# Seven half-size products in place of eight for the gate and value matmuls of an attention + two-MLP kernel

## The chip, the cores and the metric

One core of a Trainium2 chip runs the whole program. The metric is the device time of one execution in microseconds (us); a kernel's time is the median of several executions. TensorE (PE in the profile) does the matmuls, VectorE (DVE) and ScalarE (ACT) the elementwise work, and SyncE (SP) issues every DMA on one queue, in order.

## The reference

```python
# attention: x (4, 8, 512, 64), state (4, 8, 32, 64), scale 1/8
a = softmax(scale * x @ state.T);   xread = a @ state
a2 = softmax(scale * state @ x.T);  sread = a2 @ x
y = concatenate([xread, sread]) -> 2176 rows of 512

# first MLP, d_ff 2048
h = y @ w_in;  y = (h * tanh(softplus(h))) @ w_out

# second MLP, d_ff 1536
xn = y / sqrt(mean(y * y) + 1e-6) * rms_g
g, v = xn @ w_gate, xn @ w_val
out = (silu(g) * v) @ w_out2
```

The weights lie in DRAM as 64-bit floats.

## The kernel before

Rows are worked on in chunks: chunks 0 to 3 are the 512 read rows of one batch each, and chunk 4 holds the 128 state rows. Activations lie transposed in SBUF (features on partitions, rows along the free dimension), four tiles of 128 features to a chunk.

Every matmul operand is an fp16 pair, a high half and a low half, and a product of two such operands is three fp16 matmuls (high by high, high by low, low by high). One output tile of 128 features by 512 rows over 512 input features is therefore 12 matmuls of 128x512. The code calls 512 columns of the hidden dimension a unit `u` (four for the first MLP, three for the second), and 128 of them an `f`.

- **Weights.** `fetch` (L514 to L550) loads half a unit of raw 64-bit words into a staging tile (1 MB to a DMA) and turns them into fp32 with a scaled copy (L449 or L453), a sign (L534), low bits (L539 or L541) and a join (L550). `norms` (L563) sums squares on ACT, `pow2` sends the sum through a one-column matmul with `ones` (L462) and computes a power-of-two scale in six small DVE steps (L468 to L473), and `split` writes the high half (L449 or L453) and the low half (L579). The value and gate weights (`whole`) are scaled by `rms_g` and prepared while the first MLP runs; they then stay in SBUF.
- **First MLP.** `group` gives, for each `f`, 12 matmuls (L869), the activation on ACT (L880), and the split of its result (high half L449 or L453, low half on DVE L884). `l2` follows one pair of `f` later: four pieces of 6 matmuls (L902) accumulate into four PSUM banks.
- **Second MLP.** `rms` normalizes a chunk. `gated` gives for each `f` 12 gate and 12 value matmuls (L991) into two PSUM banks, SiLU on ACT (L1000), the product with the value on DVE (L1002), and the split (L451 or L449, then L1006). `l3` (L1020) multiplies the result with `w_out2`.
- **PSUM.** Four banks `p` rotate for everything that is computed, four banks `a` hold the accumulations of `l2` and `l3`.

The order of the work is not the order of the code. Each step is an `op` with its engines, its estimated cost, what it reads and writes, and for matmuls a time `at` by which it is due; `Plan.order` simulates the engines and buffers forward and backward a few times and keeps the best order. What comes out is one fixed instruction stream for each engine, and each engine works through its stream strictly in order.

Of the kernel before, what the change touches and what calls it, by code (L numbers as in the profile page):

```python
# [21 lines left out]
XEXP = 15  # L22
TABLES = {
# [7 lines left out]
class Op:  # L31
    __slots__ = (
        "engs", "fn", "deps", "succ", "bufs", "tab", "at", "due", "reserve", "lat", "name")


class Plan:
# [15 lines left out]
    def __init__(self, nc):  # L52
        self.nc = nc
# [14 lines left out]
    def op(self, engs, fn, r=(), w=(), tab=None, at=None, reserve=0, lat=0.0, after=(), due=None, name=""):  # L68
        o = Op()
        o.engs, o.fn, o.tab, o.at, o.due, o.reserve, o.lat, o.name = engs, fn, tab, at, due, reserve, lat, name  # L70
        o.succ, o.bufs = [], []
# [68 lines left out]
    def chains(self):  # L140
# [7 lines left out]
        for o in reversed(self.ops):  # L148
            cost = min(o.engs.values())
            cost = cost + o.lat if "T" in o.engs else (1.0 if "D" in o.engs else self.SPARE) * cost + o.lat  # L150
            t = min(x for x in (o.at, o.due, 1e9) if x is not None)
            t = min([t, *(late[after[b]] - cost for b in o.bufs if b in after)])
            late[o] = min([t, *(late[s] - cost - 0.14 for s in o.succ)])
# [161 lines left out]
def attn_moe_moe_kernel(  # L315
# [27 lines left out]
    wts = ctx.enter_context(tc.tile_pool(name="wts", bufs=1))  # L343
    slots = ctx.enter_context(tc.tile_pool(name="slots", bufs=1))
    wk = ctx.enter_context(tc.tile_pool(name="wk", bufs=1))
    psum = ctx.enter_context(tc.tile_pool(name="psum", bufs=1, space=PSUM))
    att = ExitStack()
    att_p = att.enter_context(tc.tile_pool(name="att", bufs=1, side="right"))
# [21 lines left out]
    tiles = {}  # L370
    for u in range(U1):
        tiles["wi", u] = wts.tile([128, 4, 512], F32, name=f"win{u}")
        tiles["wo", u] = wts.tile([128, 4, 512], F32, name=f"wout{u}")
    for u in range(U2):
        tiles["wg", u] = wts.tile([128, 4, 512], F32, name=f"gate{u}")
        tiles["w2", u] = tiles["wi", u]
    spare = {w: wts.tile([128, 2, 512], F16, name=f"spare_{w}") for w in ("wi", "wo")}
    stage0 = wts.tile([128, 4, 512], F32, name="stage0")
    slot = [slots.tile([128, KD, 512], F32, name=f"slot{c}") for c in range(B)]
    slot.append(slots.tile([128, KD, B * NS], F32, name="slot4"))  # L380
    slot += [tiles["wg", 1], tiles["wg", 2]]
    width = [S] * B + [B * NS]
# [6 lines left out]
    P.fifo.update(("s", "g", "xb", "xt", "t2", "t3", "sbt"))  # L389
    P.pool("s", [wk.tile([128, 2, 512], F32, name=f"s{k}") for k in range(3)])  # L390
    P.pool("g", [wk.tile([128, 2, 2, 512], F16, name=f"g{k}") for k in range(3)])
    P.pool("sx", [wk.tile([128, 512], F32, name=f"sx{k}") for k in range(2)])
    P.pool("junk", [wk.tile([128, 2, 512], U8, name="junk")])
    P.pool("raw", [stage0, tiles["wg", 0]])
    P.pool("xb", [att_p.tile([128, 4, DM], F32, name="xb")])
    P.pool("xt", [att_p.tile([128, 2, 512], F32, name=f"xt{k}") for k in range(2)])
    P.pool("t2", [att_p.tile([128, 512], F32, name=f"t2{k}") for k in range(4)])
    P.pool("t3", [att_p.tile([128, 512], F32, name=f"t3{k}") for k in range(2)])
    P.pool("sbt", [att_p.tile([128, 2, 2, 128], F32, name="sbt")])
    sb = att_p.tile([128, B, 2, 4, D], F32, name="sb")  # L400
    srt = slot[B]
    P.pool("raw2", [])
    att_tiles = [0]
# [13 lines left out]
    def place(c, d):  # L417

        return reg("wg", c - B, d) if c > B else [("slot", c, d)]

    def reg(w, u, k):

        w = "wi" if w == "w2" else w
        return [(w, u, 2 * k), (w, u, 2 * k + 1)]

    def where(w, u, k, a):

        if a:  # L430
            return w, u, k, 0
        if k > 1:
            return w, u, k - 2, 1
        return ("wv", U2 - 1, k + 2, 1) if (w, u) == ("wg", 0) else (w, u - 1, k + 2, 1)

    def part(w, u, k, a):
        w, u, k, h = where(w, u, k, a)
        return half(tiles[w, u])[:, k, h, :] if u >= 0 else spare["wi" if w == "w2" else w][:, k - 2, :]

    def part_name(w, u, k, a):  # L440
        w, u, k, h = where(w, u, k, a)
        return reg(w, u, k)[h]

    def parts(w, u, ks):
        return [part_name(w, u, k, a) for k in ks for a in range(2)]
# [12 lines left out]
    def pow2(part, pname, k, floor, nm):  # L458
# [8 lines left out]
        def fn(e):  # L467
            nc.vector.tensor_scalar(t, P[b][:, :k], floor, 2.0, ALU.max, ALU.mult)  # L468
            nc.vector.tensor_scalar(q, t.bitcast(I32), 24, None, ALU.logical_shift_right)
            nc.vector.tensor_scalar(z, q, -1, 190 + XEXP, ALU.mult, ALU.add)  # L470
            nc.vector.tensor_scalar(s.bitcast(I32), z, 23, None, ALU.logical_shift_left)
            nc.vector.tensor_scalar(q, q, 64 - XEXP, None, ALU.add)
# [29 lines left out]
    def fetch(w, u, pool="raw", after=()):  # L502

        if not wide:
            op({"D": 2.95}, lambda e: nc.sync.dma_start(out=tiles[w, u], in_=source(w, u)),
               w=[n for k in range(4) for n in reg(w, u, k)], lat=1.9, after=after, name=f"load {w}{u}")
            return
        for v in range(2):
            r = buf(fresh("raw"), pool)

            def raw(r=r):
# [4 lines left out]
                w=[r, *reg(w, u, 2 * v), *reg(w, u, 2 * v + 1)], lat=1.9, after=after, name=f"load {w}{u}{v}")  # L516
            for j in range(2):
                k = 2 * v + j
                g = reg(w, u, k)

                def hi(e, raw=raw, j=j, k=k):
                    a = raw()[:, j, :].bitcast(F32).rearrange("p (f w) -> p f w", w=2)[:, :, 1]
                    copy_to(e, tiles[w, u][:, k, :], a, 2.0 ** -112)

                last = op({"A": a_sb(512), "V": v2(512)}, hi, r=[r], w=g, after=after, name=f"hi {w}{u}{k}")
# [22 lines left out]
                def join(e, k=k, q=q):  # L548
                    ti = tiles[w, u][:, k, :].bitcast(I32)
                    nc.vector.scalar_tensor_tensor(  # L550
                        ti, ti, 3, P[q].bitcast(I32), ALU.logical_shift_left, ALU.bitwise_or)

                op({"V": v1(512)}, join, r=[q, (q, "s"), (q, "l"), *g], w=g, name=f"join {w}{u}{k}")

    def norms(w, u, part, pname, gain=None):

        step = 1 if gain is not None else 2
        for k in range(0, 4, step):
            q = buf(fresh("junk"), "junk")

            def fn(e, k=k, q=q):
                jk = P[q][:, :step, :]
                nc.scalar.activation(  # L563
                    jk, tiles[w, u][:, k:k + step, :], ACTF.Square,
                    scale=1.0 if gain is None else gain[:, k:k + 1],
                    accum_out=part[:, k // step:k // step + 1])

            op({"A": a_sb(512 * step) + 0.17}, fn,
               r=["rg", *(n for j in range(step) for n in reg(w, u, k + j))], w=[q, (pname, k)], name=f"sq {w}{u}{k}")

    def split(w, u, scale, sname):

        for k in range(4):
            g = reg(w, u, k)
            hn, ln = part_name(w, u, k, 0), part_name(w, u, k, 1)
            op({"A": a_sb(512) + 0.09, "V": v2(512) + 0.06}, lambda e, k=k: copy_to(
                e, part(w, u, k, 0), tiles[w, u][:, k, :], scale(k)),
# [575 lines left out]
```

## Time and profile before

| | |
|---|---|
| median of 3 runs | 832.39 us (832.09 to 832.92) |
| profiled execution, its own time | 832.4 us |
| its span, first to last instruction | 830.6 us |
| TensorE busy | 805.8 us, 97% of the span |
| VectorE busy | 452.4 us, 54% |
| ScalarE busy | 344.2 us, 41% |
| mean granted TensorE clock | 0.989 of full speed |
| DMA | 45.26 MB, 54 GB/s over the span |

The span and the time differ by 1.8 us, which lies around the instructions. A busy time is the union of the instructions' durations on one engine. Matmuls overlap in the records, so a matmul's pace is the time of a long run of them divided by their number, not the duration of one.

### The profile page before, as it was taken

The numbers are of one execution on the slowest core, as the hardware profiler recorded it, in microseconds if no ns is written. First come the engines' busy times: TensorE is split into PE (matmuls) and PEld (weight loads), VectorE is DVE, ScalarE is ACT, GpSimd is POOL, SyncE is SP. The second block draws the span as 40 slices with busy tenths as digits, with TensorE's granted clock in tenths as the row PEclk, the third lists the DMA queues.
The fourth block names the chain that finished last, engine by engine and source line by source line (L and its number), as shares of the span: only waits on it lengthen the run. The fifth ranks groups of instructions, "written<-read, shape, count | busy, mean of one in ns | idle before, by whom it ended". The sixth has DMA issues, their size and how long they took to land.

```text
span 830.6 us, 10926 instructions
## 1 busy us (share of the span) xinstructions
PE 805.8 (97%) x4486; PEld 393.7 (47%) x4486; DVE 452.4 (54%) x962; ACT 344.2 (41%) x582; POOL 1.6 (0%) x7
## 2 busy tenths in 40 slices
PE   7689999999999999999999999999999999999996
PEld 4334444444445448644444444444444444444474
DVE  5899987459275688558884271324333352312231
ACT  5999995135152499448752140103113130100010
POOL 0000000000000000000000000000000000000000
PEclk9799999999999999999999999999999999999999
DMA  8711861000000177213100000100010000100001
GB/s 215 204 52 54 284 221 52 1 1 0 1 1 1 51 253 254 102 51 102 51 0 1 1 1 0 52 1 1 0 45 7 1 0 1 51 1 0 1 2 64
DMA packets 28517, 45.26 MB, mean 54 GB/s; under 512 B 19124, under 2 KB 19124, under 8 KB 27956
## 3 DMA queue, kind: packets, MB, share of 16 engines
q1 hardware_dynamic: 28468, 44.57, 16.4%
q8 instruction: 35, 0.57, 0.3%
q14 instruction: 14, 0.11, 0.0%
HBM read 40.11 MB, written 4.46 MB: 54 GB/s over the span
## 4 chain that ended last, share of the span: by engine, by line
PE 90%; ACT 5%; DVE 3%; SPq 1%; issue 1%; DMA 0%; ACTq 0%
PE p L991 32%; PE a L902 20%; PE p L869 19%; PE a L1020 16%; PE p L698 1%; ACT t L449 1%; ACT L282 1%; ACT slot L449 1%; ACT sx L539 1%; PE p L685 0%; SPq L653 0%; PE p L945 0%; ACT junk L563 0%; DMA xb<-in_x_dram 0%; ACT win L449 0%
## 5 line engine op out<-in xcount | busy, mean ns | idle before, releaser
L902 PE MATMUL a<-g,wout 128*128 128x512 f16 (+1 forms) x880 | 174.3, 347 | 0.0
L869 PE MATMUL p<-slot,win 128*128 128x512 f16 (+1 forms) x880 | 173.0, 347 | 0.0
L1002 DVE SCALAR_TENSOR_TENSOR s<-s,page,p 128x512 f32<-128x512 f32 x51 | 38.1, 747 | 217.2 <-PE p L991 217.2
L991 PE MATMUL p<-slot,val 128*128 128x512 f16 (+1 forms) x720 | 150.0, 347 | 0.0
L1000 ACT ACTIVATE s<-p,page 128x512 f32<-128x512 f32 x51 | 35.0, 686 | 263.3 <-PE p L991 263.2
L1020 PE MATMUL a<-win,g 128*128 128x512 f16 x544 | 136.5, 379 | 0.0
L991 PE MATMUL p<-slot,gate 128*128 128x512 f16 (+1 forms) x640 | 129.4, 347 | 0.0
L869 PEld LDWEIGHTS <-win 128*128 128x128 f16 x880 | 79.0, 98 | 83.3 <-issue 0.8
L902 PEld LDWEIGHTS <-wout 128*128 128x128 f16 x880 | 79.0, 98 | 81.9 <-issue 1.3
L991 PEld LDWEIGHTS <-val 128*128 128x128 f16 x720 | 65.2, 98 | 68.2
L1020 PEld LDWEIGHTS <-g 128*128 128x128 f16 x612 | 59.7, 98 | 72.3 <-issue 1.7
L880 ACT ACTIVATE s<-p,page 128x512 f32<-128x512 f32 x68 | 46.1, 680 | 99.5 <-PE p L869 99.5
L991 PEld LDWEIGHTS <-gate 128*128 128x128 f16 x640 | 57.7, 98 | 60.6
L453 DVE TENSOR_SCALAR g<-s,page 128x512 f16<-128x512 f32 x52 | 25.1, 483 | 60.9 <-ACT s L880 60.6
L884 DVE SCALAR_TENSOR_TENSOR g<-s,page,g 128x512 f16<-128x512 f32 x68 | 50.9, 748 | 4.4 <-ACT g L449 2.6
L1006 DVE TENSOR_TENSOR g<-s,g 128x512 f16<-128x512 f32 x51 | 35.3, 692 | 1.8 <-ACT g L449 0.2
L539 ACT ACTIVATE sx<-stage 128x512 uint16<-128x512 uint16 x41 | 31.1, 775 | 0.1
L282 ACT ACT_TABLE_LOAD x21 | 26.9, 1283 | 0.4
L449 ACT ACTIVATE slot<-a,page 128x512 f32<-128x512 f32 (+2 forms) x21 | 13.9, 676 | 24.5 <-PE a L1020 18.6
L534 DVE TENSOR_SCALAR sx<-stage 128x512 uint16<-128x512 uint16 x52 | 21.4, 455 | 4.0 <-DMA stage<-in_moe_w_val_dram 1.8
L1020 PE MATMUL a<-spare_wi,g 128*128 128x512 f16 x68 | 23.0, 379 | 0.0
L902 PE MATMUL a<-g,spare_wo 128*128 128x512 f16 (+1 forms) x80 | 20.8, 347 | 0.0
(176 smaller groups left out, 697.3 us busy)
## 6 DMA issues: line engine op xcount, KB each, us to landing
stage<-in_moe_w_out_dram SPq DMA_DIRECT2D x10, 1024.0 KB, 4.9
stage<-in_moe_w_val_dram SPq DMA_DIRECT2D x6, 1024.0 KB, 5.0
stage<-in_moe_w_gate_dram SPq DMA_DIRECT2D x6, 1024.0 KB, 5.0
stage<-in_moe_w_in_dram SPq DMA_DIRECT2D x4, 1024.0 KB, 5.5
gate<-in_moe_w_in_dram SPq DMA_DIRECT2D x4, 1024.0 KB, 6.3
gate<-in_moe_w_out_dram SPq DMA_DIRECT2D x4, 1024.0 KB, 5.1
out_dram<-slot SPq DMA_DIRECT2D x4, 1024.0 KB, 4.0
xb<-in_x_dram SPq DMA_DIRECT2D x24, 128.0 KB, 3.7
```

The source lines that it names most:

```text
L282: self.nc.scalar.preload_act_table_set(TABLES[table])
L449: nc.scalar.activation(o, i, ACTF.Copy, scale=1.0 if scale is None else scale)
L539: nc.scalar.activation(s16[:, :, 0], r16[:, :, 1], ACTF.Copy, scale=2.0 ** -13, bias=2.0 ** -14 - 0.5)
L869: nc.tensor.matmul(P[ph][:, i * n:(i + 1) * n], part("wi", u, k, a)[:, f * 128:(f + 1) * 128], xh[:, k, b, :], start=m == 0, stop=m == 3 * ...
L880: op({"A": a_ps(512) + 0.09}, lambda e, s=s, q=q, ph=ph, ce=ce: nc.scalar.activation(P[s][:, q, :], P[ph], ACTF.Mish, scale=ce), r=[ph, s, ...
L884: op({"V": v1(512) + 0.06}, lambda e, q=q, s=s, g=g, u=u: nc.vector.scalar_tensor_tensor(P[g][:, q, 1, :], P[s][:, q, :], rho[u], P[g][:, ...
L902: nc.tensor.matmul(P[ya[d]][:, :n], part("wo", u, f, a)[:, d * 128:(d + 1) * 128], P[g][:, q, b, i * n:(i + 1) * n], start=first and m == ...
L991: nc.tensor.matmul(P[p][:, i * n:(i + 1) * n], part(w, u, k, a)[:, f * 128:(f + 1) * 128], xh[:, k, b, :], start=m == 0, stop=m == 3 * KD - 1)
L1000: op({"A": a_ps(512) + 0.09}, lambda e, s=s, pg=pg: nc.scalar.activation(P[s][:, 0, :], P[pg], ACTF.Silu, scale=c3), r=[pg, "c3"], w=[s], ...
L1002: op({"V": v1(512) + 0.06}, lambda e, s=s, pv=pv: nc.vector.scalar_tensor_tensor(P[s][:, 0, :], P[s][:, 0, :], kap, P[pv], ALU.mult, ALU.m ...
L1006: op({"V": v1(512)}, lambda e, s=s, g=g: nc.vector.tensor_tensor(P[g][:, 0, 1, :], P[s][:, 0, :], P[g][:, 0, 0, :], ALU.subtract), r=[s], ...
L1020: nc.tensor.matmul(P[oa[t]], P[g][:, 0, a, o:o + 128], part("w2", u, f, b), start=first and m == 0, stop=last and m == mm - 1)
```

## The change

For chunks 0 to 3, `gated` now computes gate and value of a unit as a product of two 2x2 block matrices. The blocks of the activations are 256 features by 256 rows, those of the weights 256 features by 256 hidden columns. The scheme needs seven products where the plain one needs eight, and sums of blocks before and after. The new function `quad` issues it: seven products of 12 matmuls of 128x256 each, collected in three PSUM banks `A`, `B_` and `C`, with one copy out of PSUM and five additions on DVE (L1100) into tiles of pool `t`. A bank takes its next product only when the addition that reads it is done.

```diff
+        product(A, "A11", W11, True)
+        op({"A": a_ps(512) + 0.09, "V": v1(512) + 0.06}, lambda e: copy_to(e, P[a1], P[A]), r=[A], w=[a1], name=f"{w} a1")
+        product(B_, "S2", T2, True)
+        add(u2, B_, a1)
+        product(C, "S1", T1, True)
+        product(A, "A12", W21)
+        product(B_, "S3", T3)
+        add(u3, B_, a1)
+        add(u3, C, u3)
+        product(B_, "A22", T4)
+        add(a1, B_, a1)
+        product(C, "S4", W22)
+        add(u2, C, u2)
+        return A, u2, a1, u3
```

One product:

```diff
+                for f in range(2):
+                    for k in range(2):
+                        for a, b in ((0, 0), (0, 1), (1, 0)):
+                            nc.tensor.matmul(
+                                P[to][:, f * 256:f * 256 + 256],
+                                part(w, u, j, a)[:, k * 256 + f * 128:k * 256 + f * 128 + 128], h[:, k, b, :],
+                                start=begin and (f, k, a, b) == (0, 0, 0, 0),
+                                stop=(f, k, a, b) == (1, 1, 1, 0), skip_group_check=True)
```

The activations' sums are made in `rms`, four subtractions or additions on DVE for each chunk, and seven blocks are split into halves where four tiles were. Chunk 4 is computed plainly as before (`gated_last`, L1166).

The weights' sums are made once. `seven` takes the place of `whole` for gate and value: it applies `rms_g`, makes four sums, and splits eight tiles of a unit where four were split. Each unit has a scale of its own. Since eight tiles of six units don't fit beside the rest, each prepared unit is written to DRAM and read back when the space of the first MLP's weights is free:

```diff
+        for k in range(4):
             op({"A": a_sb(512) + 0.09, "V": v2(512) + 0.06}, lambda e, k=k: copy_to(
+                e, dst(k), dst(k), rg[:, k:k + 1]), r=["rg"], w=dn(k), name=f"gain {w}{u}{k}")
...
+        s = norms([(both(W11, W12), qn(W11, W12)), (both(W21, W22), qn(W21, W22))], (w, u), XW, f"{w}{u}")
+        for t, a, b in ((T1, W12, W11), (T3, W22, W12), (T2, W22, T1), (T4, W21, T2)):
+            op({"V": v1(512)}, lambda e, t=t, a=a, b=b: nc.vector.tensor_tensor(q(t), q(a), q(b), ALU.subtract),
+               r=qn(a, b), w=qn(t), name=f"sum {w}{u}{t}")
+        for j in range(8):
+            split(m, at, j, s, ((w, u), "s"), f"{w}{u}")
...
+    def keep(w, u, after):
+        P.spare = KEEP
+        n = 2048 if w == "w2" else 4096
+        t = dram.tile([128, n], F32, name=f"kept_{w}{u}")
+        kept[w, u] = t
+        if w == "w2":
+            plain(w, u, prep, 0, XEXP, "raw2", after)
+        else:
+            seven(w, u, prep, 0, "raw2", after)
+        op({"D": n / 690}, lambda e: nc.sync.dma_start(out=t[:, :], in_=prep(0, n)),
+           r=prep.names(0, n), w=[("kept", w, u)], lat=1.9, name=f"keep {w}{u}")
...
+        op({"D": n / 690}, lambda e: nc.sync.dma_start(out=m(at, n), in_=kept[w, u][:, :n]),
+           r=[("kept", w, u)], w=m.names(at, n), lat=1.9, after=after, name=f"back {w}{u}")
```

SBUF is laid out anew as a few large regions (`Mem`), with dependencies kept by 1 KB pieces. All nine late units are prepared in one region, `prep`, and through one staging tile (there were two). The first MLP's work is put in another sequence: attention of chunk 2 moves behind most of the work on chunks 0 and 1, and the order of the chunks changes.

```diff
-        attention(2, T0 + DUE2)
...
-        group(0, 0, [0], None, B + 1)
-        group(1, 1, [0], None, B + 2)
-        group(2, 2, [0], None, 3)
...
+        group(0, 0, [0], None, 2)
+        group(1, 1, [0], None, 3)
+        group(2, 0, [1], 2, 2)
+        group(3, 1, [1], 3, 3)
+        group(4, 0, [2, 3], 2, 0)
+        flush()
+        attention(2, clock[0] + DUE2)
+        group(5, 1, [2, 3], 3, 1)
+        flush()
         attention(3, clock[0] + DUE3)
...
+        for u in range(U2):
+            for w in ("wg", "wv"):
+                keep(w, u, [bar])
+        for u in range(U2):
+            keep("w2", u, [bar])
...
+        group(6, 2, every, None, 2)
+        flush()
+        rms(0, slots_xe[0], [conv, done])
+        group(7, B, every, None, B)
+        group(8, 3, every, None, 3)
```

How the streams move is shown at three places. The first is DVE in the middle of the first MLP, where value and gate weights are prepared. `psm` is the region of `prep`, `page` holds scales, `g` and `tt` belong to the first MLP's results. Before, while units of `val` are made:

```order
L550 SCALAR_TENSOR_TENSOR val_2300<-val_2300,sx_109 128x512
L453 TENSOR_SCALAR g_107<-s_104,page_137 128x512
L884 SCALAR_TENSOR_TENSOR g_107<-s_104,page_137,g_107 128x512
L534 TENSOR_SCALAR sx_110<-stage_89 128x512
L534 TENSOR_SCALAR sx_109<-stage_89 128x512
L541 TENSOR_SCALAR sx_110<-stage_89 128x512
L550 SCALAR_TENSOR_TENSOR val_2301<-val_2301,sx_110 128x512
```

With the change, the end of one unit's sums and its scale:

```order
L918 SCALAR_TENSOR_TENSOR g<-tt,page_116,g 128x512
L544 TENSOR_SCALAR sxm<-psm 128x512 x2
L459 TENSOR_SCALAR psm<-psm 128x2x256
L551 TENSOR_SCALAR sxm<-psm 128x512
L560 SCALAR_TENSOR_TENSOR psm<-psm,sxm 128x2x256 x2
L918 SCALAR_TENSOR_TENSOR g<-tt,page_116,g 128x512
L638 TENSOR_TENSOR psm<-psm 128x512 x2
L578 TENSOR_TENSOR page_110<-page_110 128x1
L638 TENSOR_TENSOR psm<-psm 128x512
L474 TENSOR_SCALAR page_110<-p_84 128x1
```

The subtractions L638 are new, and between the sum of squares (L578) and the scale (L474) stands the one-column matmul on PE, at a fixed place of PE's stream.

The second is DVE in the second MLP. Before, one `f` after the other, with a step of `rms` between:

```order
L1002 SCALAR_TENSOR_TENSOR s_105<-s_105,page_138,p_98 128x512
L940 TENSOR_TENSOR rms_2296<-rms_2296,rms_2297 128x512
L1006 TENSOR_TENSOR g_108<-s_105,g_108 128x512
L1002 SCALAR_TENSOR_TENSOR s_103<-s_103,page_138,p_97 128x512
L451 CAST g_106<-s_103 128x512
L1006 TENSOR_TENSOR g_106<-s_103,g_106 128x512
```

With the change (`p_83` to `p_86` are the four banks, `tt` the tiles of pool `t`):

```order
L1138 TENSOR_TENSOR g<-tt,g 128x512 x3
L457 COPY tt<-p_84 128x512
L1100 TENSOR_TENSOR tt<-p_85,tt 128x512 x2
L1100 TENSOR_TENSOR tt<-p_83,tt 128x512
L1100 TENSOR_TENSOR tt<-p_85,tt 128x512
L1100 TENSOR_TENSOR tt<-p_83,tt 128x512
L457 COPY tt<-p_86 128x512
L1100 TENSOR_TENSOR tt<-p_84,tt 128x512
```

The copy and the additions stand between products that reuse the same bank.

The third is SP's queue. Before, raw weights alternate between two staging tiles (`stage_89`, and `gate_84` or later `stage_2303`):

```order
L514 DMA stage_89<-in_moe_w_in_dram 128x2x1024
L514 DMA gate_84<-in_moe_w_in_dram 128x2x1024
L514 DMA stage_89<-in_moe_w_out_dram 128x2x1024
L514 DMA gate_84<-in_moe_w_out_dram 128x2x1024
L514 DMA stage_89<-in_moe_w_val_dram 128x2x1024
L514 DMA stage_2303<-in_moe_w_val_dram 128x2x1024
```

With the change (`kept_` names are in DRAM):

```order
L525 DMA psm<-in_moe_w_gate_dram 128x2x1024 x2
L525 DMA psm<-in_moe_w_val_dram 128x2x1024
L1241 DMA kept_wg_106<-psm 128x4096
L525 DMA psm<-in_moe_w_val_dram 128x2x1024
L525 DMA psm<-in_moe_w_gate_dram 128x2x1024
L1241 DMA kept_wv_107<-psm 128x4096
L525 DMA psm<-in_moe_w_gate_dram 128x2x1024
```

A unit's write to DRAM stands in the same queue between the loads of the next unit's two halves.

## Rows read from the trace of the kernel before

**Rows 1.** The page: span, busy time of each engine, share of the chain by engine.

```profile
span 830.6 us, 10926 instructions
PE 805.8 (97%) x4486; PEld 393.7 (47%) x4486; DVE 452.4 (54%) x962; ACT 344.2 (41%) x582; POOL 1.6 (0%) x7
PE 90%; ACT 5%; DVE 3%; SPq 1%; issue 1%; DMA 0%; ACTq 0%
```

**Rows 2.** Busy time by stretch: stretch and its length, then each engine's busy time.

```profile
core 0: us, PE busy (x) PEld busy (x) DVE busy (x) ACT busy (x) POOL busy (x), PEclk, DMA share, GB/s
0.00:14.00 14.00, 10.96 (x64) 7.54 (x64) 4.15 (x8) 4.79 (x11) 1.59 (x7) 0.88 0.72 187
14.00:122.20 108.20, 94.30 (x608) 45.83 (x609) 99.55 (x241) 101.34 (x185) 0.00 (x0) 0.95 0.55 166
...
420.00:791.00 371.00, 371.00 (x1717) 168.50 (x1716) 136.16 (x232) 75.53 (x112) 0.00 (x0) 1.00 0.02 9
...
799.00:815.00 16.00, 16.00 (x253) 14.47 (x251) 5.17 (x8) 2.75 (x4) 0.00 (x0) 1.00 0.17 68
```

**Rows 3.** The chain that ended last, second MLP: start us, length us, what.

```profile
783.34 2.59 PE p L991 x12
...
809.60 5.36 PE p L991 x96
814.96 7.78 PE a L1020 x36
```

**Rows 4.** Groups by form: busy us, mean ns of one, then idle before.

```profile
L991 PEld LDWEIGHTS <-val 128*128 128x128 f16 x720 | 65.2, 98 | 68.2
...
L1002 DVE SCALAR_TENSOR_TENSOR s<-s,page,p 128x512 f32<-128x512 f32 x51 | 38.1, 747 | 217.2 <-PE p L991 217.2
L1006 DVE TENSOR_TENSOR g<-s,g 128x512 f16<-128x512 f32 x51 | 35.3, 692 | 1.8 <-ACT g L449 0.2
L453 DVE TENSOR_SCALAR g<-s,page 128x512 f16<-128x512 f32 x52 | 25.1, 483 | 60.9 <-ACT s L880 60.6
L550 DVE SCALAR_TENSOR_TENSOR win<-win,sx 128x512 int32<-128x512 int32 x28 | 18.4, 684 | 0.9 <-ACT sx L539 0.3
...
L483 DVE TENSOR_SCALAR page<-page,page 128x1 f32<-128x1 f32 x52 | 8.9, 202 | 0.0
...
L563 ACT ACTIVATE junk<-win 128x1024 uint8<-128x1024 f32 x14 | 14.7, 1052 | 3.5 <-DVE win L550 3.5
L449 ACT ACTIVATE win<-win,page 128x512 f16<-128x512 f32 x18 | 12.6, 719 | 7.6 <-DVE win L579 7.5
L449 ACT ACTIVATE win<-stage 128x512 f32<-128x512 f32 x19 | 12.2, 671 | 0.0
```

**Rows 5.** Timeline of PE, start of the first MLP: start us, length us, instructions.

```profile
42.30 0.66 PE L685 MATMUL p<-ident,xb 128*128 128x128 f32 x4
...
50.78 0.60 PE L869 MATMUL p<-slot,spare_wi 128*128 128x512 f16 x2
```

**Rows 6.** Timeline of DVE, the scale of the third weight unit.

```profile
102.70 0.16 DVE L468 TENSOR_SCALAR page<-p 128x1 f32<-128x1 f32 x1
```

**Rows 7.** DMA issues: KB each, us to landing.

```profile
stage<-in_moe_w_val_dram SPq DMA_DIRECT2D x6, 1024.0 KB, 5.0
...
out_dram<-slot SPq DMA_DIRECT2D x4, 1024.0 KB, 4.0
```

**Rows 8.** Timeline of all engines: a hand-over from PE to DVE.

```profile
658.00 2.75 PE L991 MATMUL p<-slot,val 128*128 128x512 f16 x12
...
660.59 0.81 PE L1020 MATMUL a<-win,g 128*128 128x512 f16 x3
660.86 0.75 DVE L1002 SCALAR_TENSOR_TENSOR s<-s,page,p 128x512 f32<-128x512 f32 x1 [5.82 <-PE p L991]
```

**Rows 9.** Timeline of all engines: a hand-over from DVE to a waiting PE.

```profile
83.88 0.75 DVE L753 SCALAR_TENSOR_TENSOR slot<-p,page,slot 128x512 f16<-128x512 f32 x1
...
84.69 0.65 PE L771 MATMUL p<-xb,t 128*32 128x64 f32 x32 [0.38 <-DVE slot L753]
```

More of the change, by code (lines that the diff above doesn't have):

```diff
@@ L415, in bank, with sl_names, part, part_names @@
         return buf(fresh("bank"), pool)
[L417 to L445, printed above, removed]
+    def sl_names(c, d):
+        return slotm[c].names(d * width[c], width[c])
+    def part(w, u, j, a):
+        m, at = rest[w, u] if j == 7 else (home[w, u][0], home[w, u][1] + 512 * j)
+        return m(at + 256 * a, 256, F16)
+    def part_names(w, u, js):
+        m, at = home[w, u]
+        return [n for j in js for n in (rest[w, u][0].names(rest[w, u][1], 512) if j == 7 else m.names(at + 512 * j, 512))]
     def copy_to(e, o, i, scale=None):
@@ L548, in join @@
                 def join(e, k=k, q=q):
-                    ti = tiles[w, u][:, k, :].bitcast(I32)
+                    ti = dst(k).bitcast(I32)
                     nc.vector.scalar_tensor_tensor(
[L551 to L558, printed above, removed]
+                        ti, ti, 3, two(P[q].bitcast(I32)), ALU.logical_shift_left, ALU.bitwise_or)
@@ L644, in attention @@
         if b == 1:
-            xb, xbl = "x1", [n for k in range(KD) for n in place(3, k)]
+            xb, xbl = "x1", [n for k in range(KD) for n in sl_names(3, k)]
             P.place[xb] = slot[3]
@@ L964, in rms @@
[L964 to L982 removed]
+            to = y[:, d, :] if c < B else t(d % 2)
@@ new lines, in quad, with product, fn, add @@
+    def quad(c, u, w):
+        A, B_, C = bank(), bank(), bank()
+        a1, u2, u3 = (buf(fresh(k), "t") for k in ("a1", "u2", "u3"))
+        blk = xblk[c]
+        def product(to, xn, j, begin=False, end=False):
+            h, hn = blk[xn]
+            def fn(e):
+                for f in range(2):
[6 more added lines that the diff above has]
+                                stop=(f, k, a, b) == (1, 1, 1, 0), skip_group_check=True)
+            cost = pe(256, 12)
+            op({"T": cost}, fn, r=[*hn, *part_names(w, u, [j])], w=[to, *(["l1"] if begin else [])],
+               at=clock[0], name=f"{w} c{c} u{u} {xn}")
+            clock[0] += cost
+        def add(to, bank_, a):
+            op({"V": v1(512) + 0.06}, lambda e: nc.vector.tensor_tensor(P[to], P[bank_], P[a], ALU.add),
+               r=[bank_, a], w=[to], name=f"{w} add")
+        product(A, "A11", W11, True)
[12 more added lines that the diff above has]
+        return A, u2, a1, u3
@@ L1019, in fn @@
                     for a, b in ((0, 0), (0, 1), (1, 0)):
                         nc.tensor.matmul(
-                            P[oa[t]], P[g][:, 0, a, o:o + 128], part("w2", u, f, b),
-                            start=first and m == 0, stop=last and m == mm - 1)
+                            P[oa[t]], P[g][:, a, o:o + 128], part("w2", u, f, b),
+                            start=first and m == 0, stop=last and m == 11)
                         m += 1
-            cost = pe(512, 3 * len(fs))
@@ L1026, in l3 @@
-            op({"T": cost}, fn, r=[g, *parts("w2", u, fs)], w=[oa[t]], at=clock[0], name=f"l3 c{c} u{u}")
+            cost = pe(512, 12)
+            rd = gs[t // 2 * 2:t // 2 * 2 + 2] if c < B else gs
+            op({"T": cost}, fn, r=[*rd, *part_names("w2", u, range(4))], w=[oa[t]], at=clock[0], name=f"l3 c{c} u{u}")
             clock[0] += cost
@@ new lines, in attn_moe_moe_kernel @@
+        load("wg", 0, [done])
+        load("wv", 0, [done])
+        for u in range(U2):
+            load("w2", u, [conv])
+        gated_scales()
+        group(6, 2, every, None, 2)
+        flush()
+        rms(0, slots_xe[0], [conv, done])
+        group(7, B, every, None, B)
+        group(8, 3, every, None, 3)
+        flush()
+        for u in range(1, U2):
+            load("wg", u)
+            load("wv", u)
+        rms(1, slots_xe[1])
+        gated(0)
+        rms(2, slots_xe[0])
```

522 lines of the change are left out of this document (312 added, 210 removed).

## The prediction

> **What bounds the kernel now.** I began with the page. TensorE is busy for 97% of the span, and 90% of the chain that ended last is PE [rows 1]. A busy PE need not be a PE at its peak, so the next view was busy time by stretch [rows 2]: from 420 to 791 us PE is busy in every microsecond at the full granted clock, while DVE is busy for 136 of 371 us and ACT for 76. The second MLP is bound by PE alone. The start is another matter. From 14 to 122 us DVE is busy for 99.6 of 108.2 us (92%) and ACT for 101.3, and PE, at 94.3, has only just enough to do. The reader should keep both stretches in mind: the change takes work from PE in the second and adds work to DVE, part of it in the first. The chain then gives PE's paces [rows 3]: 12 matmuls of 128x512 in 2.59 us, 215.8 ns each, and 96 of 128x128 in 5.36 us, 55.8 ns each. Each of these matmuls loads weights of its own; a load lasts 98 ns [rows 4], longer than the 55.8 ns between two matmuls, so the loads lie beside the matmuls.
>
> The profiled execution took 832.4 us with a span of 830.6, and the median of the runs is 832.39: the sum below starts from 832.4 and needs no correction.
>
> **What PE saves: 28.5 us.** Removed are 4 chunks x 3 units x 2 weights x 4 `f` x 12 = 1152 matmuls of 128x512, 248.6 us at 215.8 ns. Added are 4 x 3 x 2 x 7 products x 12 = 2016 of 128x256. No steady run of that width is in the trace. The two paces of [rows 3] lie on a line of 0.4167 ns a column plus 2.5 ns, which gives 109.2 ns at 256 columns and 220.1 us. As PE was never idle there, all 28.5 us are on the path. Everything else on PE has the same count as before.
>
> The Trainium skill, page "TensorE: Matmul & The Clock Gate", section "Back-to-back issue gap", states about 81 ns for each pair of weight load and matmul at 128 columns, 25 ns above its figure without the load. By an estimate from that page, 25 ns on each of the 2016 narrow matmuls would cost 50 us and turn the gain into a loss of 22. The trace disagrees: 55.8 ns at 128 columns, loads included [rows 3].
>
> **What DVE gets.** Six units of gate and value each get four multiplications by the gain (on DVE or ACT), four subtractions and four more splits. In the second MLP, 24 calls of `quad` bring 120 additions and 24 copies out of PSUM, and `rms` 4 sums and 3 more splits a chunk. With 0.69 us for an addition (L1006), 0.75 for a low half and 0.48 for a high half on DVE [rows 4], that is about 150 us more DVE work, 452 to about 600. In total there is room for it beside PE; where it stands decides.
>
> **First MLP, start: 12 us lost.** Take the place in PE's stream where the one-column matmul for the first gate unit's scale stands. Everything behind it waits until DVE has delivered the sum of squares. On PE, from the first L1 matmul to this place, stand 20 groups of 12 (51.8 us), 192 matmuls of the second layer (41.4) and attention pieces: 44 transposes at 0.165 us [rows 5] and some 6 us of smaller ones. With the first matmul at 50.8 as before [rows 5] (the work ahead of it on DVE is about the same), PE is there at 50.8 + 106.5, some 157 us. On DVE 375 instructions stand ahead of it: 140 of 0.66 to 0.75 us (100), 58 of 0.45 to 0.48 (27), 176 small ones of 0.15 to 0.25 (30), and memsets (2), 159 us. Priced like that, the 249 instructions of before up to 122.2 come to 109.4 where the trace shows 103.7 busy [rows 2], so 159 becomes 151. With 4.2 of it done by 14 us, and the rest at 92% as in [rows 2], DVE is there at 14 + 146.5/0.92 = 173, 16 us behind PE; without any idle time at 161, 4 behind. As a check on the kernel before: ahead of its third weight unit's scale stand 88 us of such durations, 83 after the same correction, which gives 14 + 79/0.92 = 100 us, and the trace shows it at 102.7 [rows 6]; PE had a third chunk's work to fill that time. With the change that chunk's attention is later, and DVE must prepare the same weights in front of less PE work. I take 12, nearer the measured 92%; the ends are 0 and 16. From there on DVE has fewer instructions to a PE group, and the lag does not grow.
>
> **First MLP, preparing: 3 us lost.** Nine units go through one region, one after the other. A gate or value unit's cycle: eight low halves and some six high halves on DVE, 6.0 + 2.9; two low halves of the first MLP between them, 1.5; the write of 2 MB, twice the 4.0 us of a 1 MB write [rows 7], 8.0; two copies and joins until the staging tile is free, 2.7; the second load, 5.0 [rows 7]; two more copies and joins, 2.7; a gain, 0.7; the second square, 1.05; the scale through PE, about 1.5. That is 32 us [rows 4, 7]. Between two such scales PE's stream has 6 groups and 12 pieces of 6 matmuls, 31 us. PE waits for each, so the preparing is as much on the path as PE itself. One microsecond for each of six cycles is 6; since a write of twice the size need not take twice the time, I take 3, with ends 0 and 12.
>
> **Second MLP: 3 us lost.** Counted in PE's new stream, 48 times only one other product (12 x 109.2 ns = 1.31 us) lies between two products into one bank, and the bank's reader must be done in that time. DVE starts 0.27 us after PE's last matmul gave way to the next [rows 8], an addition takes 0.69 to 0.75, and a PE that waits starts 0.06 after DVE's end [rows 9]: 1.02 to 1.08, which leaves 0.23 to 0.29. So it fits where DVE is free, and not where another instruction of 0.7 us has just begun. At worst each of the 48 loses 0.45, 22 us; at best nothing. DVE is busy for some 60% of this stretch, mostly in the order in which PE delivers, so I take 3. The reads back from DRAM, 1.8 MB each, have tens of microseconds until use and cost nothing; were that cover gone, each would show at up to twice the 5.0 us of a 1 MB load [rows 7]. The tail after the last 36 matmuls [rows 3] is unchanged.
>
> **Sum.** 832.4 - 28.5 + 12 + 3 + 3 = 821.9. I forecast **822 us**, 814 to 830 for this case alone.
>
> **Rivals.**
> - *The lag at the start is absorbed.* DVE runs denser when PE waits for it, at the 4 us end or below, and the other two terms stay near 0: 832.4 - 28.5 + 4 = 808. For it: PE and DVE at 87 and 92% side by side up to 122 us. Against: three chunks were interleaved there, now two.
> - *Slower: the preparing through DRAM sets the pace.* One staging tile and one region leave no load under the splits of the unit before. If a cycle is 36 us instead of 32, eight cycles after the first cost 32, not 3: 851. It turns the result slower from 1.7 us a cycle. Against it: ACT and DVE have gaps in that stretch, and the hand-overs of [rows 9] are short.
> - *Slower: the additions hold PE up.* At the upper end of the third loss, 22 instead of 3: 841; from 0.27 us for each of the 48 it eats what is left of the gain. Against it: the 0.23 us to spare.
> - *Narrow matmuls cost more than their columns.* If a quarter of each 98-ns load were exposed, 50 us more: 872. Against it: 55.8 ns at half that width [rows 3], and a granted clock of 1.00 from 799 to 815 us, where most of the 253 matmuls are 128 wide [rows 2].
>
> That the matmuls are not saved is no rival: PE's changed stream holds the 2016.
>
> **Chances.** The forecast's case 0.56, the absorbed lag 0.22, the preparing 0.10, the additions 0.08, narrow matmuls 0.02, and 0.02 for what I don't see. About 0.2%, 1.7 us, can be told from no change. The forecast's case gives 0.53 to faster and 0.03 to same; the absorbed lag 0.22 to faster; the slower rivals reach their weak ends, too, and give 0.02 to faster and 0.03 to same; the rest, 0.17, is slower. The range from 807 to 838 leaves out the strong ends: below, a gain with no loss at all (804), above, most of the two slower rivals.
>
> **What would show it.** Right: a run of L1088 matmuls at 12 in 1.31 us; PE idle of some 12 us between 50 and 180 us, released by DVE; DVE busy about 600 us; few PE waits after 430. Wrong: PE waiting at L468 again and again from 180 to 420 (the preparing); waits at L1088 released by L1100 (the additions); L1088 at more than 1.4 us (narrow matmuls). A start without idle time on PE would put it at the lower end.

## The result, and the profile after

The changed kernel takes **811.25 us**, median of four runs (810.59 to 811.83); the kernel before took 832.24 (830.2 to 832.92) beside it. The ratio is 0.9751, 95% interval 0.9733 to 0.977: 21 us faster, where 10 were forecast. The profiled execution took 811.83 us with a span of 810.1.

The page of the changed kernel: span, busy time of each engine, chain by engine, and the costliest DVE group.

```profile
span 810.1 us, 13000 instructions
PE 784.5 (97%) x5362; PEld 481.5 (59%) x5362; DVE 596.1 (74%) x1237; ACT 373.9 (46%) x617; POOL 1.6 (0%) x7
...
PE 69%; DVE 12%; ACT 9%; DMA 8%; issue 1%; SPq 0%; ACTq 0%; DVEq 0%
...
L1100 DVE TENSOR_TENSOR tt<-p,tt 128x512 f32<-128x512 f32 x120 | 82.5, 689 | 80.4 <-PE p L1088 79.8
```

DVE has 596.1 us of work where it had 452.4 [rows 1], as the prediction had it (600); the 120 additions cost 82.5 of that. PE is still busy 97% of a shorter span. The chain has fallen from 90% PE to 69%: it now runs through other engines for almost a third of the time, and that isn't yet a loss, as the next view shows.

Busy time by stretch, columns as in [rows 2]:

```profile
0.00:14.00 14.00, 12.08 (x68) 8.19 (x68) 5.25 (x10) 5.96 (x12) 1.59 (x7) 1.00 0.71 194
14.00:58.40 44.40, 33.29 (x209) 17.55 (x208) 42.70 (x116) 43.83 (x84) 0.00 (x0) 0.69 0.69 206
58.40:122.20 63.80, 63.35 (x391) 29.96 (x390) 61.43 (x150) 61.08 (x108) 0.00 (x0) 1.00 0.42 140
122.20:182.00 59.80, 59.59 (x355) 29.27 (x354) 55.81 (x187) 42.53 (x78) 0.00 (x0) 1.00 0.21 64
182.00:290.00 108.00, 108.00 (x504) 48.74 (x503) 95.55 (x187) 54.14 (x85) 0.00 (x0) 1.00 0.40 151
290.00:420.00 130.00, 126.03 (x882) 69.98 (x881) 94.02 (x194) 68.58 (x107) 0.00 (x0) 1.00 0.47 172
420.00:791.00 371.00, 371.00 (x2871) 271.21 (x2870) 238.25 (x396) 97.10 (x146) 0.00 (x0) 1.00 0.09 36
```

PE is idle for 0.7 us between 58 and 290, for 4.0 between 290 and 420, and never in the second MLP from 420 to 791, although DVE's work there has grown from 136 to 238 us.

The chain that ended last, second MLP (start us, length us, what):

```profile
642.58 10.36 PE a L1200 x48
...
710.34 14.41 PE p L1088 x132
...
786.36 8.04 PE p L1166 x144
794.40 7.78 PE a L1200 x36
```

These are the three paces: 215.8 ns at 512 columns, 14.41/132 = 109.2 at 256, 55.8 at 128, each matmul with a weight load of its own. The 109.2 that stood on a line between the two others is exact, and the tail of 36 [rows 3] is as before. The Trainium skill, page "TensorE: Matmul & The Clock Gate", section "Back-to-back issue gap", gives about 81 ns at 128 columns and 131 at 512 as sustained spacing and treats the line as that of an isolated matmul; here the line holds in long runs, and the trace disagrees with both figures.

Waits of PE (waited for: us in total, times, longest), the row of the scale matmul, and its count:

```profile
PE p L468 <- DVE page L578: 4.0, 3, 1.5
```

```profile
L468 PE MATMUL p<-page,ones x38: 167/250/352, 12.7 to 444.0; 128*128 128x1 f32 x36, 128*128 128x4 f32 x2
```

### The profile page after: what moved, and what is told of

Same layout as the page of the kernel before. It is cut to its first block, busy times and chain, and to the rows that moved or that the text cites. A ratio compares the mean times of both kernels' runs of the same rounds, so it can differ in the third digit from the quotient of the medians.

```text
span 810.1 us, 13000 instructions
## 1 busy us (share of the span) xinstructions
PE 784.5 (97%) x5362; PEld 481.5 (59%) x5362; DVE 596.1 (74%) x1237; ACT 373.9 (46%) x617; POOL 1.6 (0%) x7
## 4 chain that ended last, share of the span: by engine, by line
PE 69%; DVE 12%; ACT 9%; DMA 8%; issue 1%; SPq 0%; ACTq 0%; DVEq 0%
PE p L1088 27%; PE a L1200 16%; PE a L940 11%; PE p L903 9%; DMA psm<-in_moe_w_out_dram 3%; PE p L1166 2%; ACT sxm L549 2%; DVE psm L590 2%; DMA psm<-in_moe_w_gate_dram 1%; DMA psm<-in_moe_w_val_dram 1%; ACT junk L574 1%; DVE g L918 1%; DVE psm L459 1%; DMA kept_wg<-psm 1%; PE a L1266 1%
## 5 line engine op out<-in xcount | busy, mean ns | idle before, releaser
L940 PE MATMUL a<-g,w2m 128*128 128x512 f16 (+1 forms) x960 | 185.7, 347 | 0.4 <-ACT slot L455 0.4
L903 PE MATMUL p<-slot,w 128*128 128x512 f16 (+1 forms) x960 | 184.7, 348 | 0.0
L1100 DVE TENSOR_TENSOR tt<-p,tt 128x512 f32<-128x512 f32 x120 | 82.5, 689 | 80.4 <-PE p L1088 79.8
L903 PEld LDWEIGHTS <-w 128*128 128x128 f16 x960 | 85.6, 98 | 91.5 <-issue 2.9
L1200 PE MATMUL a<-psm,g 128*128 128x512 f16 x612 | 138.0, 379 | 0.0
L940 PEld LDWEIGHTS <-w2m 128*128 128x128 f16 x960 | 85.7, 99 | 87.8 <-issue 3.1
L1088 PEld LDWEIGHTS <-w2m 128*128 128x128 f16 x672 | 65.7, 98 | 11.3
L1088 PEld LDWEIGHTS <-w 128*128 128x128 f16 x672 | 65.7, 98 | 11.2 <-issue 1.7
L1088 PEld LDWEIGHTS <-attm 128*128 128x128 f16 x672 | 65.7, 98 | 10.3
L918 DVE SCALAR_TENSOR_TENSOR g<-tt,page,g 128x512 f16<-128x512 f32 x68 | 50.7, 748 | 3.0 <-ACT g L455 2.1
L1088 PE MATMUL p<-slot,attm 128*128 128x256 f16 x384 | 46.5, 273 | 0.0
L1088 PE MATMUL p<-slot,w2m 128*128 128x256 f16 x384 | 46.3, 273 | 0.0
L455 ACT ACTIVATE psm<-psm,page 128x512 f16<-128x512 f32 (+1 forms) x37 | 26.2, 717 | 30.4 <-DVE psm L590 23.4
```

The lines of the kernel that those rows point to most:

```text
L455: nc.scalar.activation(o, i, ACTF.Copy, scale=1.0 if scale is None else scale)
L903: nc.tensor.matmul(P[ph][:, i * n:(i + 1) * n], part("wi", u, k, a)[:, f * 128:(f + 1) * 128], xh[:, k, b, :], start=m == 0, stop=m == 3 * ...
L918: op({"V": v1(512) + 0.06}, lambda e, s=s, g=g, u=u: nc.vector.scalar_tensor_tensor(P[g][:, 1, :], P[s], rho[u], P[g][:, 0, :], ALU.mult, ...
L940: nc.tensor.matmul(P[ya[d]][:, :n], part("wo", u, f, a)[:, d * 128:(d + 1) * 128], P[g][:, b, i * n:(i + 1) * n], start=first and m == 0, ...
L1088: nc.tensor.matmul(P[to][:, f * 256:f * 256 + 256], part(w, u, j, a)[:, k * 256 + f * 128:k * 256 + f * 128 + 128], h[:, k, b, :], start=b ...
L1100: op({"V": v1(512) + 0.06}, lambda e: nc.vector.tensor_tensor(P[to], P[bank_], P[a], ALU.add), r=[bank_, a], w=[to], name=f"{w} add")
```

## The experiments

The theory after the result: the saving of 28.5 us is whole; the start costs next to nothing, because DVE keeps ahead of PE by a small margin; what is given back is mostly the preparing, some 4 us; the additions are covered. The rivals: DVE still holds PE up at the start (the forecast's lag, only smaller); part of the saving itself is missing; DVE, not the transfer, paces the preparing. Times are medians, to be held against 811.25; the kernel before took 830.8 to 831.7 beside them.

### The eighth product back

```diff
             def fn(e):
+                for z in range(1 + (xn == "S4")):
                     for f in range(2):
```

> The changed kernel with the S4 product run twice into its bank in each of the 24 groups, in the same order of all else: eight products where the change has seven, all additions kept. The output isn't the reference's: that product counts twice. Theory: TensorE sets the second MLP and its additions are covered, so 24 x 12 x 109.2 ns = 31.4 us, less up to 1 us of small waits that the longer group covers: 841.5 to 843. Rival: the additions or banks already held TensorE up by several us in the changed kernel: 832 to 839.

Measured: 841.66 us, ratio to before 1.0117 (1.0095 to 1.0138): 30.4 us for 288 matmuls, 105.6 ns each where the pace is 109.2. The second MLP's first product and its last matmul (the times are the first and last start of a group), as changed and then with the product back:

```profile
L1088 PE MATMUL p<-slot,attm x384: 270/273/273, 411.3 to 701.0; 128*128 128x256 f16 x192
L1200 PE MATMUL a<-psm,g x612: 378/380/380, 468.5 to 801.8; 128*128 128x512 f16 x153
```

```profile
L1089 PE MATMUL p<-slot,attm x384: 271/273/273, 407.9 to 722.6; 128*128 128x256 f16 x192
L1201 PE MATMUL a<-psm,g x612: 378/380/380, 470.5 to 830.0; 128*128 128x512 f16 x153
```

That is 390.5 and 422.1 us, 31.6 more: a product left out is worth its whole time here, and the additions and banks take nothing back that shows. The microsecond that the two times lack was won ahead of it: from 290 to 420 us PE is idle for 2.0 us in this profile and for 4.0 in the one as changed.

A first try, eight plain products with two to a bank and no additions, told nothing:

```diff
-        A, B_, C = bank(), bank(), bank()
+        cs = [bank() for _ in range(4)]
...
+        for b, (x0, w0, x1, w1_) in zip(cs, (("A11", W11, "A12", W21), ("A11", T1, "A12", W22),
+                                            ("S1", W11, "A22", W21), ("S1", T1, "A22", W22))):
+            product(b, x0, w0, True)
+            product(b, x1, w1_)
```

> The changed kernel with eight plain products of halves in place of seven, 96 of 256 columns more for each of the 24 groups' eighth product in all (24 x 12 = 288), and none of the additions of results; the weights' sums, the kept copies and the memory as changed. The output isn't the reference's: the block of the right-hand weights that isn't resident is replaced by a sum, and one activation block by another. Theory: TensorE sets the second MLP, so 288 x 109.2 ns = 31 us slower than the changed kernel, about 842.5 (841 to 844), and 10 us slower than the kernel before, which is what the preparing and the narrow products cost. Rival: the additions hold TensorE up by some us, so less comes back: 836 to 840.

Measured: 871.95 us, 1.0486 (1.0457 to 1.0515). The planner ordered all engines anew, and one scale, which PE reached at 439 us, came 20 us late, two thirds of what it took beyond the forecast (timeline of PE in that kernel):

```profile
458.94 0.58 PE L468 MATMUL p<-page,ones 128*128 128x1 f32 x2 [19.99 <-DVE page L578]
```

So an experiment here must keep the order of the three compute engines. The ones below do, but for the first two with the kept copy in pieces.

### More and less work on DVE ahead of the first gate unit's scale

Eight or 24 needless operations on a tile `spin` of 128x512 of their own, in the second (and the third and fourth) units' splits of the first MLP's weights; and the opposite, 16 low halves that are only set to zero.

```diff
+        def low(e):
+            if who in ("wi1", "wo1"):
+                nc.vector.tensor_tensor(spin, spin, spin, ALU.max)
+            nc.vector.scalar_tensor_tensor(lo, f, s, h, ALU.mult, ALU.subtract)
```

```diff
+            if who in ("wi1", "wo1", "wi2", "wo2"):
+                nc.vector.memset(lo, 0.0)
+            else:
+                nc.vector.scalar_tensor_tensor(lo, f, s, h, ALU.mult, ALU.subtract)
```

> The changed kernel with 8 needless VectorE operations of 128x512 numbers (0.69 us each, 5.5 us) among the first MLP's splits of its second units, in the same order of all else. VectorE was busy 140.5 of the 146 us between 14 and 160 us and ended the first gate unit's scale 1.4 us before TensorE came for it. Theory (VectorE has no more room than that): 5.5 - 1.4 = 4 us slower, about 815. Rival (its 5.5 idle us can take work): 811 to 812.

> The same with 24 such operations (16.6 us), among the splits of the second, third and fourth units of both weights. Theory: 16.6 - 1.4 = 15 us slower, about 826. Rival (the 5.5 idle us take work too): 16.6 - 1.4 - 5.5 = 10 us, about 821. If the prediction's lag at the start was wrong in kind and VectorE isn't waited for there, 811 to 813.

> The changed kernel with 16 of the first MLP's splits (second and third units of both weights) cut short on VectorE: the low half is set to zero and not computed from 512 numbers, in the same order of all else. The output isn't the reference's: those low halves are left out. That takes some 16 x 0.5 = 8 us from VectorE before the first gate unit's scale. 8 operations more had cost 2.8 us of their 5.5, so VectorE was near its limit. Theory (the start isn't waited for in the changed kernel, VectorE ends 1.4 us ahead): 810 to 811.5, as the changed kernel. Rival (VectorE still holds TensorE up by some us there, as the prediction's lag would): 804 to 808.

Measured: with 8 more 814.0 us (0.9787, 0.9767 to 0.9806), 2.8 slower; with 24 more 821.99 (0.9882, 0.9863 to 0.9901), 10.7 slower; with 16 cut short 809.67 (0.9731, 0.9715 to 0.9747), 1.6 faster by the medians, within the intervals of the two ratios. Busy time from 14 to 160 us with 16 cut short, as changed, and with 24 more, one kernel to a fence:

```profile
14.00:160.00 146.00, 131.05 (x854) 65.84 (x853) 135.32 (x375) 138.06 (x257) 0.00 (x0) 0.94 0.49 149
```

```profile
14.00:160.00 146.00, 134.23 (x846) 66.52 (x845) 140.47 (x369) 137.22 (x255) 0.00 (x0) 0.91 0.48 150
```

```profile
14.00:160.00 146.00, 125.95 (x809) 62.66 (x809) 142.53 (x371) 130.90 (x239) 0.00 (x0) 0.92 0.46 142
```

DVE is 93%, 96% and 98% busy (third busy time of a row). Of 16.6 us added 5.9 found room, somewhat more than the 5.5 that were idle, so the rival of an elastic DVE holds at 24, and at 8 the result lies between the two. Of the work cut short PE got nothing back: in that run PE is busy 63.37 and 59.80 of the 63.8 and 59.8 us that follow 58.4, as good as all of it, where the changed kernel had 63.35 and 59.59. Its profiled run is 1.2 us shorter (810.68 and 811.83), and by as much its first L1 matmul comes earlier (47.79 us, not 49.03), ahead of the first work cut short, at 64 us; the granted clock from 14 to 58 us was 0.81 there and 0.69 as changed. DVE isn't waited for on the way to the scale, but its margin is a few microseconds. Where the added work does make PE wait, it isn't at the scale of the forecast (waits of PE from 58 to 182 us with 24 more; L807 and L820 belong to the attention, L908 is the first layer):

```profile
PE p L807 <- DVE attm L458: 3.1, 1, 3.1
PE p L908 <- DVE page L475: 2.8, 1, 2.8
PE p L820 <- ACT attm L456: 2.2, 1, 2.2
```

### The kept copy written twice

```diff
+        def put(e):
+            nc.sync.dma_start(out=t[:, :], in_=prep(0, n))
+            if w != "w2":
+                nc.sync.dma_start(out=t2[:, :], in_=prep(0, n))
```

> Each kept copy of a gate or value unit written twice, to two places in DRAM, same order of all else. Theory: the write is a link of the chain through the one region, whose cycle (32 us) is already TensorE's (31 us): each of six cycles grows by about 7.5 us, less some 2 us of lead in all, 35 to 45 us slower, 846 to 856. Rival: the write lies beside other work, 811 to 816.

Measured: 839.84 us, 1.0099 (1.0069 to 1.0129): 28.6 slower, under the theory's 35 and far above the rival. SyncE's queue as changed, then with the copy doubled: from the write's issue to that of the next load, which waits until the region is free.

```profile
193.54 0.35 SPq L1241 DMA_DIRECT2D kept_wg<-psm  x1
201.26 0.37 SPq L525 DMA_DIRECT2D psm<-in_moe_w_val_dram  x1
```

```profile
194.35 0.35 SPq L1243 DMA_DIRECT2D kept_wg<-psm  x1
194.75 0.42 SPq L1245 DMA_DIRECT2D kept_wg<-psm  x1
208.31 0.38 SPq L525 DMA_DIRECT2D psm<-in_moe_w_val_dram  x1
```

14.0 us where it was 7.7. In the same queue the six gaps grow by 6.2, 4.9, 4.9, 4.0, 4.5 and 3.3 us, 27.8 in all and not the 45 that 7.5 a cycle would make. In the waits of PE it is the scale that pays:

```profile
PE p L468 <- DVE page L578: 23.7, 7, 5.6
```

That is 19.7 us more than the 4.0 as changed, so the write is a link of the chain, and the chain had some 8 us of room over the whole preparing, more than the 2 expected. The rest of the 28.6 us isn't waiting: PE was busy for 793.2 us where it was 784.5, with the same 5362 matmuls, and in the two stretches with these waits its granted clock, 1.00 as changed, was 0.97 and 0.95:

```profile
182.00:290.00 108.00, 99.70 (x453) 44.11 (x450) 82.02 (x157) 46.11 (x72) 0.00 (x0) 0.97 0.45 180
290.00:420.00 130.00, 115.31 (x791) 64.76 (x792) 90.85 (x185) 61.84 (x96) 0.00 (x0) 0.95 0.49 193
```

### The kept copy in halves and quarters

The chain of waits as changed shows the links one after the other: the last split's low half, the write, a conversion, the next load.

```profile
322.79 0.76 DVE psm L590
323.60 7.84 DMA kept_wg<-psm
331.52 0.70 ACT psm L455
332.24 5.08 DMA psm<-in_moe_w_val_dram
```

A first pair gave the planner transfers of half or quarter size to place:

```diff
+        for lo in range(0, n, 2048):
+            op({"D": 2048 / 690}, lambda e, lo=lo: nc.sync.dma_start(
+                out=t[:, lo:lo + 2048], in_=prep(lo, 2048)),
...
```

> The changed kernel with each prepared unit written to DRAM in halves, each as soon as its own blocks are split, not in one transfer at the end. Theory: the 5 us that TensorE lost between 316 and 402 us (it waits at the scale of a unit, 1.0 to 1.5 us shown at each of three) come from a chain through one region, load, conversion, splits, write, in which the 7 to 8 us write is the last link; with halves only about 4 us of the write is left behind the last split, the cycle falls from 32 to about 28 us, under TensorE's 31, and the waits go: about 806.5 us (805.5 to 808). Rival: VectorE's work, not the transfer, sets the cycle: 810.5 to 812.

> The same in quarters: about 2 us of the write behind the last split. Theory: no more than in halves, as TensorE's 31 us then bound the cycle already: 806 to 807.5. If the cycle is still bound by the chain with halves, quarters give 1 to 3 us more. Rival (VectorE sets the cycle): 810.5 to 812.

Measured: 815.25 us (0.9809, 0.9785 to 0.9834) and 816.42 (0.9812, 0.9792 to 0.9831), slower than the change. Both have other orders on all engines. With halves the waits for DVE's sum at the scale did fall, from 4.0 to 1.3 us (with quarters they rose to 5.7), but PE lost 5 us elsewhere, as its stretch shows:

```profile
122.20:182.00 59.80, 54.81 (x391) 27.57 (x390) 56.69 (x167) 44.84 (x71) 0.00 (x0) 1.00 0.14 36
```

So the pair tells of the planner's order, not of the write. The second pair issues the early pieces from within the split and leaves the other engines' streams as they were:

```diff
+            if put is not None:
+                put(512 * (j + 1))
...
+            def put(hi):
+                if hi % 2048 == 0 and hi < n:
+                    nc.sync.dma_start(out=t[:, hi - 2048:hi], in_=prep(hi - 2048, 2048))
```

> The kept copy in halves again, but with the instructions of TensorE, VectorE and ScalarE in exactly the changed kernel's order: only SyncE's queue has six transfers more, the first half's issued when the fourth of eight blocks is split. (In the first try with halves the planner moved TensorE's scale matmuls and the kernel took 814 to 815 us with 1.3 us of waits left at a scale.) Theory: the write is the last link of the preparing chain, about 4 us of it go from each cycle, the 4.0 us that TensorE waits at a scale go with it: 807 (806 to 808.5). Rival: the 5 us over 316 to 402 us aren't the chain's: 810.5 to 812.

> The same in quarters, same order of the three engines. Theory: TensorE's own 31 us a unit bound the cycle with halves already, so no more than with halves: 806 to 808. Rival: 810.5 to 812.

Measured: 807.45 us (0.9708, 0.969 to 0.9726) and 807.12 (0.9703, 0.9686 to 0.9721): some 4 us faster than the change, whose interval (from 0.9733) lies just above theirs, and as expected no more from quarters. With halves, PE's waits at a scale and the stretch from 290 us:

```profile
PE p L468 <- DVE page L578: 0.9, 1, 0.9
```

```profile
290.00:420.00 130.00, 129.00 (x897) 71.59 (x896) 93.58 (x195) 67.44 (x106) 0.00 (x0) 1.00 0.46 172
```

Idle time there fell from 4.0 to 1.0 us; with quarters it was 1.6, and 2.0 to 3.8 in the six other profiles with the whole copy written once and the change's order. DVE's own work is the same (93.58 and 94.02 us), so the rival falls. In the profiles the scale at 212.14 us comes 1.4 us earlier to begin with, and the last one, at 443.96, 4.8: 3.4 us are the preparing's in this pair. (From the one scale to the other it is 228.5 us with halves and 229.1 with quarters, 230.3 to 232.8 in the profiles with whole copies, written once, and seven products.)

But 4 us did not go from each cycle, as the theory had it. From the last write's issue to the next load SyncE's queue has 7.5, 6.8, 7.9, 8.0 and 7.0 us for the first five units with halves, and 7.7, 7.1, 7.6, 8.0 and 8.6 with whole copies. Of the six writes only the fifth holds DVE up for long, 4.87 us as changed (timeline of DVE) and 2.02 with halves (the row in the last section):

```profile
331.46 0.43 DVE L459 TENSOR_SCALAR psm<-psm 128x512 f32<-128x512 f32 x1 [4.87 <-DMA kept_wg<-psm]
```

So the whole write held up the preparing near its end, where PE has its waits, and the 807 was met with a smaller saving at fewer places than forecast. This version beats both kernels.

### A second read of the bank before the additions

```diff
+                if bank_ == B_:
+                    nc.vector.tensor_tensor(spin, P[bank_], P[a], ALU.add)
                 nc.vector.tensor_tensor(P[to], P[bank_], P[a], ALU.add)
```

The second kernel does this only where `to` is `u3`, behind the S3 product.

> A second VectorE read of the bank (0.69 us) ahead of each of the 72 additions that read the bank of the S2, S3 and A22 products, result unused. Theory: a product of 1.31 us leaves 0.25 us of room at one or two places of each of the 24 groups, so 0.44 us is lost at 24 to 48 of them: 10 to 21 us slower, 822 to 832. Rival: VectorE, busy 238 of the 371 us, has room everywhere: 811 to 813.

> Of the 72 second reads of a bank that made the kernel 10.4 us slower, only the 24 ahead of the addition after the S3 product are left, the one place of a group where the next product of the same bank comes a single product (1.31 us) later. Theory (the room is short at this place alone): about the same 10 us, 820.5 to 822.5. Rival (the longer VectorE queue did it, or the other places share it): a third to a half of it, 814 to 817.

Measured: 821.67 us (0.9886, 0.9864 to 0.9908), 10.4 slower for 72 reads, and 813.3 (0.9775, 0.9761 to 0.979), 2.0 slower for 24. The 2.0 is no more than the two intervals can tell. The first agreed with the low end of the theory, and the second showed that it agreed by chance: the one short place costs 0.09 us each, not 0.44, and even less than the rival's third. Stretch 420 to 791 us with 72, then with 24 reads:

```profile
420.00:791.00 371.00, 363.99 (x2717) 261.52 (x2715) 278.27 (x462) 95.84 (x145) 0.00 (x0) 1.00 0.08 31
```

```profile
420.00:791.00 371.00, 369.65 (x2836) 269.02 (x2835) 250.46 (x417) 97.37 (x146) 0.00 (x0) 1.00 0.09 33
```

PE is idle there for 7.0 and 1.35 us; DVE has 75% and 68% of the stretch, as against 64%. The 72 cost 0.14 us each and these 24 0.09, so the one place that the theory named isn't where the room is short. That it is DVE's in-order queue, which bunches behind a group, fits but wasn't tried apart.

## Why the prediction was right in sign and wrong in size

- **What PE saves, 28.5 us: right.** 109.2 ns to the last digit, and the eighth product put back lengthens the second MLP by 31.6 us where 31.4 were expected. One thing was overlooked: PE's other work isn't quite the same. There are 38 one-column matmuls for scales where there were 26, two for each of six more scales; PE is held 0.14 us by such a pair (rows below, 160.07 to 160.21), 0.8 us.
- **"First MLP, start: 12 us lost": the step that failed.** DVE was to reach the sum for the first gate unit's scale at 173 us and PE the scale at 157. The changed kernel, DVE's busy time up to there, then DVE's timeline, then PE's:

```profile
0.00:158.70 158.70, 144.42 (x375) 0.91 0.50 155
```

```profile
158.69 0.16 DVE L578 TENSOR_TENSOR page<-page 128x1 f32<-128x1 f32 x1
```

```profile
160.07 0.28 PE L468 MATMUL p<-page,ones 128*128 128x1 f32 x2
160.21 1.02 PE L940 MATMUL a<-g,w2m 128*128 128x512 f16 x4
```

  PE's place was met within 3 us. DVE's 375 instructions took 144.4 us, not 151; 139.2 of them after 14 us, which at 92% would have brought it there at 165. So the sum of the durations was 7 us too long, and at 92% DVE would have been 5 us behind PE and not 16. The other 6.6 us are density: from 14 us on DVE was busy for 139.2 of 144.7 us, 96%. Its sum was done 1.2 us ahead of PE, so no lag came about. That is the rival "the lag at the start is absorbed", against which the prediction held that only two chunks were interleaved. The 92% was what DVE happened to be asked for, not what it can do: the runs with less and more work had it at 93 and 98%. "A start without idle time on PE" was the sign named for the lower end, and from 58 us on it is what the stretches show. What the start did cost, some 3 us, is of another kind (the sum, below).
- **"Preparing, 3 us lost": right.** PE waits 4.0 us at three scales; halves took 3.4 to 3.8 back, and doubling the write cost 28.6. The slower rival in which it sets the pace fell: the chain had some 8 us of room, and from 181 to 377 us the scales came 31.2 to 34.0 us apart, 31.2 or 33.2 where PE did not wait.
- **"Second MLP, 3 us lost": nothing that shows.** PE is busy throughout, the chain runs 132 matmuls without a gap, and an eighth product costs its whole time. The 22 us that the upper end allowed don't show; but 72 more reads of 0.69 us cost 10, so the room is not wide.
- **The sum.** 832.4 - 28.5 + 0.8 (scales) + 4.0 (preparing) = 808.7, with 811.8 measured in the profiled run. The 3 us left lie ahead of 122 us, and the prediction has no term for them: TensorE's clock. PE's busy time fell by 21.3 us (805.8 to 784.5), 6.4 less than the 27.7 that its changed matmuls save. From 14 to 58 us the granted clock, which has levels of 1.2 and 2.4 GHz, was 0.69 on average (second row of the stretches above), and in the kernel before 0.88:

```profile
14.00:58.40 44.40, 31.54 (x253) 16.18 (x253) 40.57 (x106) 42.09 (x87) 0.00 (x0) 0.88 0.60 161
```

  By an estimate from these rows (busy time times what the clock lacks of 1.00, from 0 to 58 us), the lower level cost 10.3 us where it cost 5.1 before, so that some 5 of the 6.4 us are the clock's. On the other side PE was idle for 13.5 us ahead of 122 us and for 16.9 before, 3.5 less. Together that is the 3 us. No run changed the clock by itself, and why it stood lower stays open; with the same order of work the mean of this stretch varied from 0.69 to 0.81 among the profiles.

## What to carry to other kernels

An engine's busy share in a stretch that another engine paces is what was asked of it, not its ceiling (DVE had 92% there before, 96 to 98% here): bound a delay by the dense case first, and take the observed share only as the other end. A transfer through one region is a link in series with what fills and what empties it, and it is worth what is waited for behind it: pieces of half the size, written as they got done, took some 4 us off the time, where 4 us from each of six cycles had been reckoned. And where a planner sets the order, compare only kernels whose other engines' streams stay the same: two edits that should have gained 4 us lost 4 to 5 by a new order.

## What the runs showed of the hardware

Halving the write about halved its time to landing, but not the wait behind it. Medians from issue to landing, as changed, then with halves:

```profile
kept_wg<-psm SPq DMA_DIRECT2D x3, 2048.0 KB, 7.0
kept_wv<-psm SPq DMA_DIRECT2D x3, 2048.0 KB, 7.9
```

```profile
kept_wg<-psm SPq DMA_DIRECT2D x6, 1024.0 KB, 4.2
kept_wv<-psm SPq DMA_DIRECT2D x6, 1024.0 KB, 3.9
```

With halves, VectorE's first operation behind the fifth unit's write:

```profile
327.17 0.43 DVE L459 TENSOR_SCALAR psm<-psm 128x512 f32<-128x512 f32 x1 [2.02 <-DMA kept_wg<-psm]
```

The last half was issued at 321.47 us (the first at 316.29), so that operation started 5.7 us after it; behind the whole 2 MB it was 7.9 us (323.60 to 331.46). From the issue of one write of 2 MB to the next load it took 7.7 us, and with a second one behind it 14.0.
